# Retention and two feed-forward blocks on one core: tables formed by products, small tiles of 64 bytes, another order of products and sums

## The chip, the cores and the metric

One core of a Trainium2 chip runs the whole program. The metric is the device time of a run in microseconds, the median over several runs. The engines are TensorE (PE, the matrix products; its weight loads are PEld), VectorE (DVE), ScalarE (ACT), GpSimd (POOL) and SyncE (SP, which here only issues DMAs). Data lie in SBUF (128 partitions); products are summed in PSUM, in eight banks of 128 x 512 fp32.

## The reference

Three stages, all in fp32: retention over blocks, a feed-forward block with a squared gate, and one whose two branches are multiplied. `w_in` is 512 x 2048, `w_a` and `w_b` are 512 x 1536.

```python
Dmask = np.where(rel >= 0, lam[:, None, None] ** rel[None, :, :], 0.0)
lam_pow = lam[:, None, None] ** (pos[None, :, None] + 1)
for b in range(nb):
    intra = np.einsum('bhic,bhjc->bhij', qb, kb) * Dmask[None]
    intra = np.einsum('bhij,bhjd->bhid', intra, vb)
    inter = np.einsum('bhid,bhde->bhie', qb * lam_pow[None], kv_state)
    out[:, :, sl] = intra + inter
    kv_state = lam_block * kv_state + np.einsum('bhsd,bhse->bhde', kb_dec, vb)
...
h = x @ w_in
g = np.where(h >= 1, h, np.where(h <= -1, 0.0, (h + 1) ** 2 / 4))
x = g @ w_out
...
return (x @ w_a) * (x @ w_b) @ w_out
```

There are 2 x 768 tokens, 8 heads of 64 features and `lam` of 8 numbers, one for each head.

## The kernel before

**Tiling.** The retention runs in 12 chunks of 128 tokens (6 for each batch; a chunk here spans two blocks of the reference). The feed-forward parts run in blocks of 512 tokens, three of them (`nb`), and in tiles of 128 x 512. Each operand of a wide product is held as two fp32r tiles, a higher part `hi` and a rest `lo` (`split`, L306); one product of such pairs is three matmuls, higher by higher, higher by lower, lower by higher (`mm3`, L324). A group of two or four pairs sums into one bank by 6 or 12 matmuls. Weights come as 8-byte words and are turned into a pair by `weight` (L515): two steps on ACT, three on DVE, an add, then `split`.

**Stages.** `ready_for(c)` forms the scores of a chunk, scales its keys and values and multiplies the scores by the masks; `attention(c)` updates the state and forms the output, which is split into the block tiles. The masks `dmask` (two, of even and odd heads) and the powers for the queries `tabq` are tables of powers of lam. To make them, `lam` comes by two DMAs (`lamp` on SP, `lamb` on the ACT queue), POOL raises it to powers (`base`, L378; `kdf`, L382, the powers for the keys), `base` goes to a small DRAM tensor `rows` behind a stretch of zeros, and four DMAs on the ACT queue (L390, L394) read it back with overlapping strides, which shifts it by one in each partition. `warm` (L397) issues bf16 matmuls on zeros, 8 ahead of the first scores and 8 behind.

Then come the first feed-forward block in four groups of 512 features (`h_bank` and `gate`, L560; from the second group on `h_banks`, which forms two blocks of tokens by seven products of sums, `seven`, in place of eight), the sums over the groups (`y_bank`, `gather`), the differences of tokens that the second block needs for its seven products (`tokens_y`, `strassen_tokens`), and the second block in six groups (`ab_banks`, then `o_bank` for each block of tokens). In group g the order is ab(2g), the o products of block 2 of the group before, ab(2g+1), the o products of blocks 0 and 1 of this group.

**The order.** No order is written out for the engines. Every operation is a step of `Plan` with its ways (an engine and a cost in us), its outputs and inputs. `deadlines` gives each step a due time from the order of PE's steps; `place` walks through time, and at each point takes of the steps that can begin first the one that is due first, PE out of its next 5 steps only. It gives each step a slot of its kind of tile: `t` (24 fp32 tiles, and 14 `early` ones until the retention ends), `r` (36 fp32r, and from then on 14 `late` ones in place of the early), `raw`, and 7 banks `ps`. A step may name the lock: two SBUF operands on DVE wait in the plan until POOL's instruction ends, and the other way round. `copy` (L300) has no lock. A PE step is placed whole, behind all its inputs. The queues are then filled in this order, and each engine runs its own in order.

**Places.** Tiles lie in SBUF one behind another, each at the next multiple of 32 bytes. In the program as built the t tiles begin at byte 1152 of a partition and the r tiles at 50304, both multiples of 64 like all that follow them up to the blocks. Behind these come nine small fixed tiles (`lamp` to `half`, of 4 or 32 bytes a partition), 32 bytes apart, 288 together; then the early, later the late tiles, from byte 189856 on, which is 32 more than a multiple of 64.

The lines that the change and the steps below touch: L34 (POOLS, SHARED), L83 (`step`), L109 (`deadlines`), L130 (`place`), L300 (`copy`), L316 (`mm`), L324 (`mm3`), L338 to L399 (the tables and `warm`), L560 (`gate`), L575 (`strassen_tokens`), L675 (`y_bank`), L682 (`o_bank`), L740 and L782 (the order of the stages).

## Time and profile before

| | |
|---|---|
| median of 3 runs | 628.84 us (628.33 to 629.57) |
| the profiled execution | 631.43 us |
| its span, first to last instruction | 629.6 us |
| PE busy | 597.4 us (95%), 3060 matmuls |
| DVE, ACT, POOL busy | 418.2, 273.3, 449.8 us |
| mean granted clock of PE | 0.988 |
| chain that ended last | PE 86%, DVE 9%, DMA 3% |

The span is cut into stretches by what limits each: a start in which PE has little to do, long stretches in which PE has no idle time, and some holes between stages. PE's busy time counts overlapping records and so is no measure of how fast it works; in a stretch without holes, length over count of matmuls is. A clock of 1.00 is 2.4 GHz, 0.50 is 1.2 GHz.

### The profile page before, as it was taken

To read this page: it belongs to the slowest core of one execution; us is meant where nothing else is said; L and a number is where in the kernel's file an instruction comes from. 1 tells how busy PE (TensorE), PEld (TensorE's weight loads), DVE (VectorE), ACT (ScalarE), POOL (GpSimd) and SP (SyncE) were. 2 spreads that over 40 slices of the span, in tenths; PEclk is the share of its full clock that TensorE was granted. 3 is DMA by queue.
4 is the path that set the end of the run, shared out by engine and by line. 5 is a ranking of instruction groups with operands and counts; after the bars stand their busy time and mean duration, and the time that the engine had idled before them with its cause. 6 is when DMAs were issued, how large, how long until landed. Compare 5 with 4: busy or idle time off the path is not lost.

```text
span 629.6 us, 8361 instructions
## 1 busy us (share of the span) xinstructions
PE 597.4 (95%) x3060; PEld 477.6 (76%) x3060; DVE 418.2 (66%) x618; ACT 273.3 (43%) x480; POOL 449.8 (71%) x385
## 2 busy tenths in 40 slices
PE   5599999999899999999997989999999999999997
PEld 3478788888688878888885868878878878878875
DVE  0588635337985798569889966295774884775544
ACT  0366545446643654355744555332432523523310
POOL 3488997489776667657989979474876867758640
PEclk9699999999999999999999989999999999999999
DMA  7977401023122211221201222102111222220005
GB/s 237 304 272 244 166 2 67 1 67 101 34 68 67 87 48 68 67 82 53 68 0 68 101 81 86 35 33 68 67 68 67 68 67 68 68 68 1 0 34 200
DMA packets 21081, 52.72 MB, mean 84 GB/s; under 512 B 2600, under 2 KB 5168, under 8 KB 21040
## 3 DMA queue, kind: packets, MB, share of 16 engines
q1 hardware_dynamic: 18568, 50.86, 23.7%
q10 hardware_dynamic: 2472, 1.32, 0.8%
q8 instruction: 24, 0.39, 0.2%
q14 instruction: 17, 0.14, 0.1%
HBM read 49.03 MB, written 3.15 MB: 83 GB/s over the span
## 4 chain that ended last, share of the span: by engine, by line
PE 86%; DVE 9%; DMA 3%; issue 1%; POOL 0%; ACT 0%; SPq 0%; ACTq 0%; DVEq 0%
PE ps L319 86%; DVE t L299 3%; DVE r L299 2%; DMA t<-rows 1%; DVE block L299 1%; DMA lamp<-in_lam 1%; DMA rows<-base 1%; DVE late L299 1%; DVE r L303 1%; DVE t L563 0%; DVE t L532 0%; DVE late L303 0%; POOL base L378 0%; DVE early L299 0%; DVE block L303 0%
## 5 line engine op out<-in xcount | busy, mean ns | idle before, releaser
L299 DVE TENSOR_TENSOR t<-t,ps 128x512 f32<-128x512 f32 (+1 forms) x246 | 160.3, 666 | 124.7 <-PE ps L319 104.1
L319 PE MATMUL ps<-r,r 128*128 128x512 f32 x740 | 210.2, 394 | 7.5 <-DVE t L299 3.4
L319 PE MATMUL ps<-block,r 128*128 128x512 f32 x718 | 188.9, 393 | 2.8 <-DVE t L299 1.4
L299 POOL TENSOR_TENSOR r<-t,r 128x512 fp32r<-128x512 f32 x99 | 131.2, 1339 | 69.1 <-ACT r L303 67.5
L299 POOL TENSOR_TENSOR t<-t,t 128x512 int32<-128x512 int32 (+2 forms) x136 | 150.3, 1121 | 40.7 <-ACT r L303 18.5
L319 PEld LDWEIGHTS ps<-r,r 128*128 128x128 f32 x740 | 138.8, 188 | 41.9 <-issue 3.9
L319 PEld LDWEIGHTS ps<-block,r 128*128 128x128 f32 x718 | 134.0, 188 | 34.2 <-DVE block L299 2.2
L303 ACT CAST r<-t 128x512 fp32r<-128x512 f32 x128 | 78.2, 619 | 124.7 <-DVE t L299 71.1
L319 PE MATMUL ps<-late,r 128*128 128x512 f32 x276 | 92.4, 396 | 0.4 <-DVE r L299 0.3
L319 PE MATMUL ps<-block,late 128*128 128x512 f32 x290 | 85.0, 394 | 0.0
L319 PEld LDWEIGHTS ps<-block,late 128*128 128x128 f32 x290 | 54.4, 188 | 13.3 <-DVE t L299 0.5
L319 PE MATMUL ps<-r,late 128*128 128x512 f32 x196 | 62.1, 396 | 1.1 <-DVE late L299 0.9
L527 DVE TENSOR_SCALAR words<-words 128x512 f32<-128x512 f32 x68 | 47.3, 696 | 23.4 <-ACT words L522 22.1
L319 PEld LDWEIGHTS ps<-late,r 128*128 128x128 f32 x276 | 51.7, 188 | 13.5 <-DVE r L299 1.1
L522 ACT ACTIVATE words<-raw 128x512 f32<-128x512 f32 x68 | 43.3, 637 | 35.9 <-DVE t L532 33.3
L303 ACT CAST late<-t 128x512 fp32r<-128x512 f32 x52 | 31.7, 618 | 54.9 <-POOL t L299 31.4
L303 ACT COPY t<-ps 128x512 f32<-128x512 f32 x49 | 28.6, 586 | 47.1 <-PE ps L319 46.6
L529 DVE TENSOR_SCALAR words<-words 128x512 int32<-128x512 int32 x68 | 47.4, 697 | 1.6
L532 DVE SCALAR_TENSOR_TENSOR t<-raw,words 128x512 int32<-128x512 int32 x64 | 43.8, 684 | 2.0
L319 PEld LDWEIGHTS ps<-r,late 128*128 128x128 f32 x196 | 37.1, 189 | 10.4 <-DVE late L299 1.3
L319 PE MATMUL ps<-late,late 128*128 128x512 f32 x120 | 40.6, 402 | 1.6 <-DVE late L303 1.0
L565 ACT ACTIVATE t<-t,half 128x512 f32<-128x512 f32 x43 | 30.5, 722 | 25.8 <-DVE t L563 25.8
(78 smaller groups left out, 520.0 us busy)
## 6 DMA issues: line engine op xcount, KB each, us to landing
raw<-in_w2ab SPq DMA_DIRECT2D x24, 512.0 KB, 3.3
t<-in_att SPq DMA_DIRECT2D x37, 256.0 KB, 5.4
raw<-in_w1i SPq DMA_DIRECT2D x16, 512.0 KB, 3.4
raw<-in_w1o SPq DMA_DIRECT2D x16, 512.0 KB, 4.7
raw<-in_w2o SPq DMA_DIRECT2D x12, 512.0 KB, 3.2
early<-in_att SPq DMA_DIRECT2D x11, 256.0 KB, 5.4
out<-t SPq DMA_DIRECT2D x8, 256.0 KB, 2.3
t<-rows ACTq DMA_DIRECT2D x2, 256.0 KB, 6.4
```

Of the source, the lines that this page charges most:

```text
L299: plan.step(ways, [o], [x, y], lambda e: engine[e].tensor_tensor(out=o(), in0=x(), in1=y(), op=op))
L303: (nc.scalar.copy if e == "ACT" else nc.vector.tensor_copy)(o(), x())
L319: nc.tensor.matmul(**{k: v() if isinstance(v, View) else v for k, v in kw.items()})
L522: lambda e: nc.scalar.activation(out=words(), in_=f_(high)(), func=ACTF.Abs), horizon)
L527: lambda e: ts_(out=words(), in0=words(), scalar1=HIGH_MIN, scalar2=HIGH_MAX, op0=ALU.max, op1=ALU.min))
L529: lambda e: ts_(out=wi(), in0=wi(), scalar1=3, scalar2=0x3FFFFFFF, op0=ALU.logical_shift_left, op1=ALU.bitwise_and))
L532: lambda e: nc.vector.scalar_tensor_tensor(out=vi(), in0=high(), scalar=-0x40000000, in1=wi(), op0=ALU.bitwise_and, op1=ALU.bitwise_or))
L565: lambda e: nc.scalar.activation(out=r(), in_=r(), func=ACTF.Square, scale=0.5, bias=half()))
```

## The change

1. **Small tiles.** Each small fixed tile is 16 columns of 4 bytes (`column`), 18 of them.
2. **Tables.** `lamp`, `rows` and the DMAs around it go. POOL makes a few powers of lam (`powers8`, three strips of 32 partitions: the powers 0 to 31, 16 times as much, and differences of 16), DVE makes tables of zeros and ones by comparing running numbers (`near`, `far`), 40 small fp32 products and one more spread the powers over the partitions (banks `f1`, `f2`, `f3`, `bt`), and DVE multiplies and adds these into `dmask` (`masks`); `tabq` is a product on POOL or DVE (`query_powers`).
3. **Fillers.** `warm(40)` makes 40 steps of two bf16 matmuls that the plan may place where PE has nothing else, until the first h product is placed; those left over are dropped. They hold one bank.
4. **Order in a group.** `mm3` takes all products of higher parts first and the right-hand lower parts last; for o products the left-hand lower parts last. Each input's due time is that of its own matmul, a group may begin ahead of inputs that only later matmuls read, and the matmuls of a group are put into the order one by one.
5. **The plan.** PE is taken from its next 12 steps; `copy` on DVE names the lock; 26 t, 40 r, 8 early and late tiles; other windows for choosing among steps; a way out where the reserve of tiles lets nothing be placed.
6. **Sums in PSUM.** The last y sums of block 2 and of half of block 1 are added into the bank and split from there; the gates of the first eight h products too; one difference of tokens is formed in the bank.
7. **o products.** Two of the four o products of block 2 move behind ab(2g+1).

```diff
-POOLS = {"t": 24, "r": 36, "raw": 4, "ps": 7}
-SHARED = 14
+POOLS = {"t": 26, "r": 40, "raw": 4, "ps": 7}
+SHARED = 8
+LOOK = 12
+SPARE, SLOPE = 2, 3.0
+AHEAD = 30
+NEAR, NEAR_PE = 0.25, 0.2
...
-                    s.before.add(self.writer[k])
+                    w = self.writer[k]
+                    s.before.add(w)
+                    s.lead[w] = min(s.lead.get(w, 1e9), leads[i] if leads else 0.0)
...
+                clock += 0.0 if s.filler else s.ways[0][1]
...
-                t = min([a.late for a in s.after] + [clock + 5, bound.get(s, 1e9)])
+                t = min([a.late + a.lead[s] for a in s.after] + [clock + 5, bound.get(s, 1e9)])
...
-        pe = deque(s for s in self.steps if s.ways[0][0] == "PE")
+        pe = deque(s for s in self.steps if s.ways[0][0] == "PE" and not s.filler)
...
-                begin = max([at[e], given] + [x.done if x.engine == e else x.end + HOP for x in s.before])
+                begin = max([at[e], given] + [x.done if x.engine == e else x.end + HOP - s.lead[x] for x in s.before])
...
+                if s.filler:
+                    yield e, begin, 99, cost, s
+                    continue
...
+                choices = [x for s in ready for x in options(s, window, False)]
+                choices = [min(choices, key=lambda x: x[2])] if choices else []
...
-            near = 0.5 if e == "PE" else 0.12
+            near = NEAR_PE if e == "PE" else NEAR
...
+            if s is ends:
+                for x in [x for x in waiting if x.filler]:
+                    drop(x)
...
-        plan.step(ways or [("ACT", act(n)), ("DVE", dve(n))], [o], [x], emit)
+        plan.step(ways or [("ACT", act(n)), ("DVE", dve(n), x.buf.kind != "ps" and o.buf.kind != "ps")], [o], [x], emit)
...
+    def mm(groups, cost, outs, ins, leads=None):
+        def product(kw):
+            return lambda e: nc.tensor.matmul(**{k: v() if isinstance(v, View) else v for k, v in kw.items()})
+        s = plan.step([("PE", cost)], outs, ins, None, leads=leads)
+        s.parts = [(cost * i / len(groups), product(kw)) for i, kw in enumerate(groups)]
+        return s
...
+    def mm3(ps, pairs, start=True, late=1):
+        kws, ins, leads = [], [], []
+        for a, b in ((0, 0), (1, 0), (0, 1)) if late else ((0, 0), (0, 1), (1, 0)):
+            for l, r in pairs:
+                ins += [l[a], r[b]]
+                leads += [WIDE * len(kws)] * 2
+                kws.append(dict(out=ps, lhsT=l[a], rhs=r[b], start=(start and not kws), stop=False, skip_group_check=not start))
+        kws[-1]["stop"] = True
...
+    def column(name, dtype=F32):
+        return View(fixed([128, 16], dtype, name))
...
+    load(lamb, bass.AP(tensor=lam.tensor, offset=lam.offset, ap=[[0, 128], [1, H]]), 4096, [("ACT", 2.2, False, 4096)])
+    small("POOL", one(qi), [], lambda: nc.gpsimd.iota(one(qi)(), pattern=[[0, 1]], base=0, channel_multiplier=1), 0.14)
...
+    def power(o, e):
+        small("POOL", o, [lamb, one(e)],
+              lambda: nc.gpsimd.tensor_tensor(out=o(), in0=lamb(), in1=one(e)().to_broadcast([128, H]), op=ALU.pow), 1.64)
...
+          lambda: ts_(out=one(keep)(), in0=one(cf)(), scalar1=16.0, scalar2=None, op0=ALU.is_ge))
+    small("DVE", powers8, [powers8, one(keep)],
+          lambda: ts_(out=powers8()[64:96], in0=powers8()[64:96], scalar1=one(keep)()[64:96], scalar2=None, op0=ALU.mult))
...
+        def equal(shift):
+            o, c = new(), column(f"c{base}_{shift}")
+            small("DVE", one(c), [one(cf)],
+                  lambda: ts_(out=one(c)(), in0=one(cf)(), scalar1=float(-shift), scalar2=None, op0=ALU.add))
+            plan.step([("DVE", dve())], [o], [whole, one(c)],
+                      lambda e: ts_(out=o(), in0=whole(), scalar1=one(c)(), scalar2=None, op0=ALU.is_equal))
...
+    equal = ones_where([[1, 4], [0, 8], [1, 16]], 1)
+    near = [equal(4 * g) for g in range(4)]
+    equal = ones_where([[1, 4], [1, 8], [0, 16]], -8)
+    far = [equal(4 * g) for g in range(2)]
...
+    f1, f2, f3, bt = (bank() for _ in range(4))
+    for o, q, sel in ((f1, 1, far), (f2, 0, near), (f3, 2, near)):
+        kws = []
+        for i in range(4 * len(sel)):
+            kws.append(dict(out=o.of(lambda t, i=i: t[:, i * H:(i + 1) * H]),
+                            lhsT=sel[i // 4].of(lambda t, i=i, q=q: t[32 * q:32 * q + 32, (i % 4) * 128:(i % 4 + 1) * 128]),
+                            rhs=rows32(powers8, q), start=True, stop=True))
+        mm(kws, 0.07 * len(kws), [o], [powers8, *sel])
+    mm([dict(out=cols(bt, 0, 192), lhsT=full.of(lambda t: t[0:64, 0:128]), rhs=spread.of(lambda t: t[0:64, 0:192]),
+             start=True, stop=True)], 0.35, [bt], [full, spread])
...
-    rows = View(Buf("fixed", Slot(dram.tile([H, PITCH], F32, name="rows"))), keys=("z", "p"))
-    rbase = rows()[0:1, 0:1]
...
+    def masks(e):
+        d = dmask[e]
+        by_r = lambda v: v()[:, 0:128].rearrange("p (r a e o) -> p e a o r", a=4, e=2, o=1)[:, e].to_broadcast(shape)
+        plan.step([("DVE", dve())], [d], [far_f, f2], lambda _: nc.vector.tensor_tensor(
+            out=quad(d()), in0=far_f()[:, 0:64].rearrange("p (i a e o) -> p e a i o", a=4, e=2, o=1)[:, e].to_broadcast(shape),
+            in1=by_r(f2), op=ALU.mult))
+        near_d = new()
+        plan.step([("DVE", dve())], [near_d], [f3, dg], lambda _: nc.vector.tensor_tensor(
+            out=quad(near_d()), in0=dg()[:, 0:8].rearrange("p (b i o) -> p b i o", b=1, o=1).to_broadcast(shape),
+            in1=by_r(f3), op=ALU.mult))
+        tt(d, d, near_d, ALU.add)
...
+        sh = [64, 4, 8, 16]
+        src = lambda: broad()[r, 0:192].rearrange("p (a e n) -> p e a n", a=4, e=2)[:, e]
+        part = View(tabq.buf, lambda t: quad(t[r]), (e,))
+        plan.step([("POOL", pool(), True), ("DVE", dve(), True)], [part], [broad], lambda q: engine[q].tensor_tensor(
+            out=part(), in0=src()[:, :, 0:8].rearrange("p a (i o) -> p a i o", o=1).to_broadcast(sh),
+            in1=src()[:, :, 8:24].rearrange("p a (o r) -> p a o r", o=1).to_broadcast(sh), op=ALU.mult))
...
     def warm(n):
-        ps = bank()
-        mm([dict(out=ps, lhsT=idle.of(lambda t: t[:, 0:128]), rhs=idle, start=True, stop=True)] * n, 0.43 * n, [ps], [idle])
+        for _ in range(n):
+            s = mm([dict(out=warm_bank, lhsT=idle.of(lambda t: t[:, 0:128]), rhs=idle, start=True, stop=True)] * 2, 0.5,
+                   [warm_bank], [idle])
+            s.filler = True
...
-    def gate(ps, ft, nb):
...
+        v = ps if in_bank else r
+        tt(v, r, ps, ALU.max, ways=[("DVE", dve(), ps.buf.kind != "ps")])
+        gt[1, ft, nb] = split(v)
...
-        gate(product_in("1i", ft, nb), ft, nb)
+        gate(product_in("1i", ft, nb), ft, nb, nb < 2)
...
-        t1, t2, t3, t4 = (new() for _ in range(4))
-        for i, o, x, y in ((1, t1, y1[0], y0[0]), (2, t2, y1[1], t1), (3, t3, y1[1], y1[0]), (4, t4, y0[1], t2)):
+        t1, t3, t4 = (new() for _ in range(3))
+        t2 = y1[1] if y1[1].buf.kind == "ps" else new()
+        for i, o, x, y in ((1, t1, y1[0], y0[0]), (3, t3, y1[1], y1[0]), (2, t2, y1[1], t1), (4, t4, y0[1], t2)):
             tt(o, x, y, ALU.subtract)
         for i, o in ((2, t2), (3, t3), (1, t1), (4, t4)):
             ts[i, j] = split(o, *(x_view(1, j) if i == 1 else ()))
...
+        if g == FF1 // 512 - 1 and (nb == 2 or nb == 1 and m >= 2):
+            tt(ps, acc[("y", nb, m)], ps, ALU.add)
+            acc["y", nb, m] = ps
+            split(ps, *x_view(nb, m))
+            return
         y = gather(("y", nb, m), ps)
-        if g == FF1 // 512 - 1 and (nb != 1 or m >= 2):
+        if g == FF1 // 512 - 1 and nb == 0:
             split(y, *x_view(nb, m))
...
         r0 = nb * TB + m * 128
-        ps = mm3(bank(), [(lhs(gt[2, f, nb], m), wt["2o", f]) for f in range(2 * g, 2 * g + 2)])
...
-    warm(8)
+    warm(40)
     ready_for(0)
-    warm(8)
...
             h_bank(j, nb)
+            if c == 4:
+                ends = next(s for s in reversed(plan.steps) if s.ways[0][0] == "PE")
...
         if g:
-            for m in range(KT):
+            for m in range(2):
                 o_bank(g - 1, 2, m)
         ab_banks(2 * g + 1)
+        if g:
+            for m in range(2, KT):
+                o_bank(g - 1, 2, m)
```

## Rows read from the trace of the kernel before

**Rows 1.** Chain of waits, 0 to 60 us: start, length, what (times in us)
```profile
1.65 6.17 DMA lamp<-in_lam
...
9.55 5.14 DMA rows<-base
...
15.24 7.77 DMA t<-rows
```

**Rows 2.** Timeline of the start: start, length, engine, line, [idle before]
```profile
4.49 1.65 POOL L382 TENSOR_TENSOR kdf<-lamb,exk 128x8 f32<-128x8 f32 x1 [3.44 <-DMA lamb<-in_lam]
...
5.33 1.16 PE L319 MATMUL ps<-t,t 64*128 64x128 f32 x16 [0.88 <-DMA t<-in_att]
...
11.89 1.78 PE L319 MATMUL ps<-t,t 128*64 128x64 f32 x32 [1.28 <-POOL t L429]
...
17.10 1.04 POOL L429 TENSOR_TENSOR early<-t,kdf 128x512 f32<-128x512 f32 x1 [1.89 <-DMA t<-in_att]
...
20.64 0.69 PE L319 MATMUL ps<-early,t 128*64 128x128 f32 x2 [6.97 <-DVE early L299]
...
23.77 1.97 PE L319 MATMUL ps<-early,t 128*64 128x128 f32 x14 [2.44 <-DVE early L299]
...
25.67 2.08 PE L319 MATMUL ps<-t,t 64*128 64x128 f32 x16
```

**Rows 3.** Windows of the start: stretch, length, busy of five engines (count), clock, DMA
```profile
20.00:25.00 5.00, 1.92 (x14) 1.52 (x15) 3.07 (x5) 1.02 (x5) 1.00 (x1) 0.50 0.87 211
...
60.00:70.00 10.00, 9.53 (x110) 7.57 (x108) 8.90 (x16) 5.85 (x15) 10.00 (x9) 1.00 0.74 262
```

**Rows 4.** Windows of six stretches that PE fills, and of 166 to 630, columns as before
```profile
95.00:157.00 62.00, 62.00 (x275) 51.32 (x275) 31.48 (x48) 32.40 (x57) 46.55 (x41) 1.00 0.17 58
168.00:224.00 56.00, 56.00 (x244) 45.52 (x243) 42.15 (x65) 28.93 (x49) 40.97 (x36) 1.00 0.21 71
228.00:316.00 88.00, 88.00 (x381) 71.20 (x380) 69.07 (x104) 47.23 (x79) 64.12 (x55) 1.00 0.18 60
370.00:410.00 40.00, 40.00 (x176) 32.68 (x175) 17.09 (x26) 20.13 (x36) 29.12 (x27) 1.00 0.20 67
...
465.00:508.00 43.00, 43.00 (x187) 34.85 (x186) 26.59 (x42) 14.48 (x26) 29.69 (x27) 1.00 0.15 49
...
563.00:607.00 44.00, 44.00 (x192) 35.68 (x192) 24.60 (x38) 12.83 (x22) 28.86 (x27) 1.00 0.00 0
...
166.00:630.00 464.00, 448.02 (x1913) 358.54 (x1912) 325.15 (x467) 192.44 (x325) 323.35 (x274) 0.99 0.19 63
```

**Rows 5.** Timeline of PE alone, about 355 us, one merged run
```profile
355.65 3.11 PE L319 MATMUL ps<-block,r 128*128 128x512 f32 x13
```

**Rows 6.** Windows around holes of PE, and 346 to 361 between them
```profile
158.00:166.00 8.00, 6.03 (x25) 4.33 (x25) 7.73 (x9) 5.21 (x9) 7.14 (x6) 1.00 0.20 67
...
330.00:346.00 16.00, 11.69 (x48) 8.39 (x47) 15.76 (x18) 7.01 (x12) 14.77 (x10) 1.00 0.19 67
346.00:361.00 15.00, 15.00 (x67) 12.27 (x66) 13.84 (x22) 8.61 (x15) 14.74 (x13) 1.00 0.29 106
361.00:365.00 4.00, 2.14 (x9) 1.16 (x8) 3.93 (x4) 0.23 (x1) 3.22 (x3) 1.00 0.00 0
365.00:370.00 5.00, 5.00 (x16) 3.91 (x17) 3.75 (x6) 2.57 (x5) 3.10 (x3) 0.66 0.31 102
...
412.00:416.00 4.00, 3.13 (x13) 1.94 (x12) 3.90 (x5) 1.24 (x2) 3.84 (x5) 1.00 0.39 131
...
559.00:562.00 3.00, 1.63 (x7) 0.75 (x6) 2.97 (x3) 1.10 (x2) 2.92 (x3) 1.00 0.86 280
```

**Rows 7.** Groups of DVE, 318 to 324 us: count, busy, mean ns
```profile
L299 DVE TENSOR_TENSOR r<-t,r 128x512 fp32r<-128x512 f32 x1 | 5.7, 5743 | 0.0
L299 DVE TENSOR_TENSOR t<-t,ps 128x512 f32<-128x512 f32 x2 | 1.4, 682 | 2.1 <-PE ps L319 2.1
```

**Rows 8.** Timeline of DVE, 505 to 513 us, one cast
```profile
509.89 1.48 DVE L303 CAST r<-t 128x512 fp32r<-128x512 f32 x1
```

198 lines of the change are left out of this document (108 added, 90 removed).

## The prediction

> **What bounds the kernel now.** I read the chain of waits first, to see which engine the end hangs on. It is TensorE (PE) nearly everywhere after 23.8 us; before that it is a chain of small transfers [rows 1]. So the time is three sums: what PE idles at the start, how long one product takes in the dense stretches, and what PE idles in holes later. I read each in its own view.
>
> The start. lamp lands at 7.8 us, a power of it on POOL takes 1.65 (as the one of lamb [rows 2]), the powers go out to DRAM (5.14) and come back as tables (7.77): the last is there at 23.0 [rows 1]. The q, k and v of the first chunk are long there: PE forms its first scores at 5.33, its first state at 11.89, and then idles until 23.77, but for two matmuls [rows 2]. lamb, which comes by one transfer, is at POOL by 4.49 [rows 2]. From 20 to 25 us the granted clock is 0.50, the lower level of 1.2 GHz, because PE did nothing from 13.7 to 20.6; the 16 score matmuls that took 1.16 us at 5.33 take 2.08 at 25.67 [rows 2, 3].
>
> The dense stretches. In a window that PE fills, length over count is the interval between products. Records overlap (0.39 us each, 0.23 apart), so a window counts some 1.7 too many. 95 to 157 us: 62.00/273.3 = 226.9 ns. Later: 56/242.3 = 231.1, 88/379.3 = 232.0, 40/174.3 = 229.5, 43/185.3 = 232.1, 44/190.3 = 231.2 [rows 4]; together 271/1171.5 = 231.3. In the fast window no product reads a `late` tile. Those lie 32 bytes off a multiple of 64; r and block tiles lie on one. A busy VectorE (DVE) is no good reason: at 355.65 thirteen products without `late` take 3.11 us, (3.11 - 0.39)/12 = 227 ns, in a stretch where DVE is busy 13.84 of 15 us [rows 5, 6].
>
> The holes. PE lacks 1.97 us in 158 to 166, 4.31 in 330 to 346, 1.86 in 361 to 365, and at the ends of four later groups 0.87 in the first, 1.37 in the last, 4.7 in the four: 12.9 us in all. Behind the third of the seven the clock falls to 0.66 for 5 us, 1.7 us more [rows 6]. Why they arise is in single instructions: a DVE subtract of two SBUF tiles took 5.74 us, while those that read a bank of PSUM took 0.68 in the same stretch, and a DVE cast that the planner took for 0.69 took 1.48 [rows 7, 8]. Both stood between two SBUF tiles while POOL worked on SBUF tiles; a bank in PSUM as source spares DVE that wait.
>
> **The start after the change.** Seven transfers go: six of the ACT queue's seven, whose lamb stays, and lamp from SP's. ACT then has only computation behind its one DMA; nothing is moved past another on SP's queue. The powers are ready at 4.49 + 1.65 [rows 2], and 0.17 for the multiply by `keep`: 6.3 us. DVE makes six is_equal tiles at some 0.68 [rows 7] with small instructions, some 5 us from 1.5 on. This multiply waits for POOL, and up to three of the is_equal tiles stand behind it in DVE's order, so they may end near 9; PE's table products wait for them, with fillers and the next scores behind. The 40 table products are 80 matmuls. No row has 8 columns of output; the nearest are 32 matmuls of 64 weight columns in 1.78 us, 56 ns each [rows 2]. I take that, 4.5 us. Below lies the planner's cost, 2.8 us (its costs for other products agree with the trace); above, twice the row for twice the columns, 8.9. The Trainium skill (TensorE: Matmul & The Clock Gate, "LDWEIGHTS") has a load cost its columns over 1.2, however few rows: 107 ns here, as an estimate 8.5 us, by which the sum below would come to 608.5, on the way to rival (b).
>
> So the products end near 11.3; then on DVE near_d, the sum and the first mask at 0.68 each, 13.4; the other half 2.0 later, 15.4; and 1 us for fillers and queues, 16.4. That is 7.4 us before 23.77. But four banks hold tables and one the fillers, so the second chunk's scores (1.16) come later than now: 5.9. Fillers hold the clock: 23.77 to 27.75 at the lower level cost 2.0; I take 1.6. **Start: -7.5**, between -3 (products 8.9, clock lost) and -11. The loads are no new limit: the third chunk's keys are at POOL by 17.10 [rows 2], before PE could use them. Fewer early tiles (8 for 14, two more t) leave 34 for 38, some 15 of them tables for a while; I cost that at nothing, as the loads run ahead, and at up to 2 us in the range.
>
> **Alignment.** Every small tile is now 64 bytes, so `late` tiles come to multiples of 64. If all products take 226.9, 4.4 ns go for each of the 1913 matmuls of 166 to 630 us [rows 4]: **-8.4**. Bounds: 0, and -9.7 at the 5.1 ns of the slowest windows.
>
> **The holes.** Moving two o banks (12 products, 12 x 0.227 = 2.7 us) behind the second ab group covers four waits that are all under 2: -4.7. If the cover were gone, they come back whole. The hole at 361 has no earlier group to draw on; a view of 12 PE steps for 5, and the lock now charged to casts, should save half of 1.86 and of the clock's 1.7: -1.8. At 330 the sums stay in PSUM: their subtract on DVE takes 0.68 for sure where one took 5.74; but subtracts that POOL did go to DVE, busy 15.76 of 16 us there [rows 6]. -2.5 of 4.31; ends 0 and -4.3. At 158: -0.7, ends +1 and -2. "Higher parts first" cuts both ways: in a group of four pairs the last pair's higher part is needed at the 4th product instead of the 10th, 6 x 0.227 = 1.4 us earlier, its lower part one product later. One y stage may wait for it: +1.3 (0 to +4). **Holes: -8.4**, between -3 and -14. Gates in PSUM put eight subtracts (5.4 us) on DVE in 60 us of attention where it is busy 0.89 [rows 3]; POOL's release frees as much, so 0.
>
> **The sum.** -7.5 - 8.4 - 8.4 = -24.3. The profiled execution ran 631.43 us, span 629.6 and 1.8 around it: 607.1 for it. The median of the runs, 628.84, is 2.6 lower: **604.5 us**, of itself 599 to 610.
>
> **Rivals.** (a) The products stay slow: the offset is not the cause but the place at the top of the partition, or something else that came with these tiles. For it: no tile elsewhere has the offset, so the two can't be told apart here. Against: block tiles right below are fast. Then +8.4: 612.9; 0.11. The Trainium skill (SBUF — State Buffer, "Specifications") gives lines of 16 bytes, of which 32 is a whole number; by that the offset costs nothing and this rival holds, but no row speaks for lines of 16. (b) The tables are as late as now, by DVE's order and slow products: only 1.5 of 7.5 gained, 610.5; 0.10. (c) New holes for old: DVE has more to do around y, and the reordered groups wait for higher parts: nothing of 8.4, 612.9; 0.08. (d) All goes to its far end, -11 - 8.4 - 14.5: 595; 0.04. (e) Slower: a group may now be started ahead of its inputs, each counted on just for its own product, and lateness on the chip then stops PE inside groups. The products form 294 groups (by the code, of 6 and 12). From (24.3 + 1.3)/294 = 87 ns a group this eats everything; at 0.1 us, with all gains kept, it gives 634; 0.04. Against it: PE waits for nothing in the six windows [rows 4], so inputs are mostly long ready. (f) Nothing of it works or it cancels: 629; 0.01.
>
> **How the numbers follow.** Forecast 0.62, rivals as above. From 597 to 615 lie the forecast, (a), (b) and (c), 0.91 before what their own spreads leave out, nearer 0.8 with it. Faster by over 0.2% (1.3 us, about what a measurement here can tell): 0.62 + 0.11 + 0.10 + 0.08 + 0.04 = 0.95; within it 0.01; slower 0.04.
>
> **What would show it.** Start: the chain has no transfer but lamb, the first dense output products of chunk 0 stand near 16 us, and the clock is 1.00 from 15 to 30. Alignment: a full window late in the run gives 227 ns a product, with `late` tiles in it; 231 means rival (a). Holes: no idle of PE over 0.3 us at the ends of the ab groups but the first; the y sums' subtracts on DVE all near 0.68. I am wrong if PE shows many idles of a tenth of a us inside groups (e), if DVE is full through 20 to 80 us with PE waiting for it, or if the first mask comes after 20 us.

## The result, and the profile after

The changed kernel takes **615.14 us**, median of 4 runs (614.73 to 615.42), beside 628.94 (628.33 to 629.57) in 4 runs of the kernel before on the same chip: a ratio of 0.978 (0.9763 to 0.9797). It is faster, as forecast, but by 13.8 us where 24.3 were forecast, and the time lies just past the far end of the range. The profiled execution took 615.42 us, its span is 613.6 (before 629.6).

The three terms of the forecast come out in one account. There are 2340 wide products (128x512 outputs). From their starts in the trace I read when the 301st begins (the start with the retention behind it), and sum for the next 2000, to 599.7 us, what each interval takes over 226.7 ns: in "products" where it follows without a gap in under 300 ns, in "holes" else (gaps, and the stretches at the lower clock behind them). The part behind the 2301st is 9.5 us in one and 9.3 in the other.

| | 301st begins | products | holes | PE ends | span |
|---|---|---|---|---|---|
| before | 134.5 | +8.2 | +19.4 | 625.0 | 629.6 |
| after | 142.1 | +4.2 | 0.0 | 609.0 | 613.6 |
| difference | **+7.6** | **-4.0** | **-19.4** | -16.0 | -16.0 |
| forecast | -7.5 | -8.4 | -8.4 | | -24.3 |

So every term was missed: the start has become worse by as much as it was to become better, products gained half, and holes gave more than twice what I counted. The profiled execution of the kernel before took 631.43 us, 2.5 more than the median; in two later forms of it that keep its order (64-byte tiles, 1248 bytes of padding) the holes come to 17.1, so some 2 of the 19.4 us seem to belong to this one execution. The chain of waits of the changed kernel (start, length, what) shows the last: behind PE's first instruction at 6.01 there is one break of over 0.1 us, before 93.70, inside the retention.

```profile
5.88 0.14 issue
6.01 62.05 PE ps L347 x592
68.06 0.01 issue
68.06 25.07 PE ps L347 x272
...
93.22 0.43 DVE t L328
93.66 0.04 issue
93.70 515.35 PE ps L347 x2276
```

The start, as the timeline of PE shows it (start, length, engine, line, operation, count, [idle before]):

```profile
6.01 2.08 PE L347 MATMUL ps<-t,t 64*128 64x128 f32 x16 [6.01 <-DMA t<-in_att]
8.02 3.58 PE L347 MATMUL ps<-powers,t 32*128 32x8 f32 x16
11.53 2.08 PE L347 MATMUL ps<-t,t 64*128 64x128 f32 x16
13.53 12.99 PE L347 MATMUL ps<-powers,t 32*128 32x8 f32 x64
26.45 1.00 PE L347 MATMUL ps<-early,t 64*128 64x192 f32 x2
27.39 5.21 PE L347 MATMUL ps<-early 128*128 128x512 bf16 x14
32.52 0.69 PE L347 MATMUL ps<-t,early 128*64 128x64 f32 x16
```

From 6.01 on PE is never idle, and yet it is late. The 80 table products take 3.58 + 12.99 = 16.6 us, 12.99/64 = 203 ns each on the mean; by their starts in the trace they follow each other in 213 ns, but for the few where one strip ends and the next begins. The 16 scores take 2.08 as in the stretch before that had the lower clock, for 1.16 at the upper [rows 2, 3]: PE works here at 1.2 GHz. The fillers, which were to hold the clock, come only at 27.39. The reason stands in DVE's timeline: the zeros that they multiply are written by its last small instruction, and DVE then waits 10.7 us for the tables:

```profile
9.65 0.27 DVE L391 MEMSET early<- 128x256 uint32 x1
20.63 1.28 DVE L486 TENSOR_TENSOR early<-t,ps 128x512 f32<-128x512 f32 x2 [10.71 <-PE ps L347]
```

Windows of PE's stretches (stretch, length, busy of PE, PEld, DVE, ACT, POOL with counts, clock, DMA) answer [rows 4]:

```profile
100.00:150.00 50.00, 50.00 (x222) 41.42 (x221) 20.64 (x31) 27.07 (x46) 43.77 (x39) 1.00 0.12 43
170.00:225.00 55.00, 55.00 (x243) 45.23 (x242) 42.27 (x63) 28.71 (x49) 42.48 (x37) 1.00 0.23 77
230.00:315.00 85.00, 85.00 (x373) 69.73 (x372) 63.34 (x99) 45.61 (x76) 62.73 (x54) 1.00 0.19 62
166.00:606.00 440.00, 440.00 (x1925) 361.37 (x1924) 287.07 (x438) 201.34 (x339) 332.72 (x288) 1.00 0.19 64
```

Counted as in the prediction, 50.00/220.3 = 227.0 ns, then 227.9 and 85/371.3 = 228.9; before it was 226.9, 231.1 and 232.0. From 166 us to the end of the wide products PE is busy all the time, at the full clock: nothing is left of [rows 6].

### The profile page after: what moved, and what is told of

It is laid out like the page before. It is cut to its first block, busy times and chain, and to the rows that moved or that the text cites. A ratio compares the mean times of both kernels' runs of the same rounds, so it can differ in the third digit from the quotient of the medians.

```text
span 613.6 us, 8555 instructions
## 1 busy us (share of the span) xinstructions
PE 602.4 (98%) x3140; PEld 494.8 (81%) x3140; DVE 389.4 (63%) x621; ACT 283.7 (46%) x498; POOL 453.2 (74%) x397
## 4 chain that ended last, share of the span: by engine, by line
PE 98%; DMA 1%; DVE 0%; issue 0%; SPq 0%; DVEq 0%
PE ps L347 98%; DMA t<-in_att 1%; DVE t L328 0%; SPq L343 0%; DVEq L971 0%; DVEq L328 0%
## 5 line engine op out<-in xcount | busy, mean ns | idle before, releaser
L347 PE MATMUL ps<-r,r 128*128 128x512 f32 x984 | 270.1, 390 | 0.0
L328 POOL TENSOR_TENSOR r<-t,r 128x512 fp32r<-128x512 f32 x152 | 195.7, 1304 | 79.6 <-ACT r L332 74.6
L347 PEld LDWEIGHTS ps<-r,r 128*128 128x128 f32 x984 | 184.8, 188 | 40.1 <-issue 0.2
L347 PE MATMUL ps<-block,r 128*128 128x512 f32 x892 | 216.3, 391 | 0.0
L347 PEld LDWEIGHTS ps<-block,r 128*128 128x128 f32 x892 | 166.8, 188 | 36.1 <-issue 0.5
L332 ACT COPY t<-ps 128x512 f32<-128x512 f32 (+3 forms) x58 | 33.0, 569 | 82.2 <-PE ps L347 81.7
L640 ACT ACTIVATE t<-raw 128x512 int32<-128x512 uint32 x66 | 41.8, 665 | 0.0
L347 PE MATMUL ps<-t,t 64*128 64x128 f32 (+3 forms) x504 | 33.3, 279 | 6.6 <-DMA t<-in_att 6.0
L347 PEld LDWEIGHTS ps<-t,t 128*64 128x64 f32 (+2 forms) x504 | 28.1, 159 | 11.8 <-issue 9.3
L347 PE MATMUL ps<-block,late 128*128 128x512 f32 x116 | 30.9, 395 | 0.0
```

Source lines behind the costliest of these rows:

```text
L328: plan.step(ways, [o], [x, y], lambda e: engine[e].tensor_tensor(out=o(), in0=x(), in1=y(), op=op))
L332: (nc.scalar.copy if e == "ACT" else nc.vector.tensor_copy)(o(), x())
L347: return lambda e: nc.tensor.matmul(**{k: v() if isinstance(v, View) else v for k, v in kw.items()})
L640: lambda e: nc.scalar.activation(out=c(), in_=low.of(lambda t: t.bitcast(U32))(), func=ACTF.Copy, scale=2.0**-29), horizon)
```

## The experiments

Times are of the same sort as above; "before" beside them was 629.39 to 630.18 throughout.

### The start

**Tables made as before.** The changed kernel with the old way through DRAM, in small tiles of 64 bytes.

```diff
-    power(powers8, ef)
...
-    f1, f2, f3, bt = (bank() for _ in range(4))
...
+    load(lamp, bass.AP(tensor=lam.tensor, offset=lam.offset, ap=[[1, H], [0, 16], [1, 1]]), 512)
...
+    rz, rp = View(rows.buf, keys=("z",)), View(rows.buf, keys=("p",))
...
+    warm_bank = bank()
```

> The changed kernel with the tables made as before: powers to DRAM and read back (small tiles stay 64 bytes, fillers stay). If the 80 table matmuls of 128 weight columns hold up the start (17 us of PE in the changed kernel), the first output products come near 24 us again instead of 32.5 and the time falls by 7 to 9 us, to 606 to 608. If the start doesn't set the end, because DVE is busy 0.88 between 40 and 92 us, it stays within 2 us of 615.

Measured: 604.73 us (604.12 to 607.84), ratio 0.9616 (0.959 to 0.9643), 10.4 us less than the changed kernel. The 301st product begins at 132.1 for 142.1, which is nearly all of it. The table part of the change, with the late fillers that it brings, is a loss of 10 us: here the zeros stand early in DVE's order again, and the first fillers run at 1.19. Its chain of waits shows that the old way is also faster here than it was before [rows 1]: 4.28 and 4.79 us for the two transfers that took 5.14 and 7.77, and PE runs from 18.64.

```profile
0.74 4.96 DMA lamp<-in_lam
...
8.64 4.28 DMA rows<-base
...
13.01 4.79 DMA t<-rows
...
18.64 203.44 PE ps L347 x1360
```

**Zeros first.** DVE writes the zeros ahead of everything else, so that fillers can run early.

```diff
-    small("DVE", idle, [], lambda: nc.vector.memset(idle(), 0.0), 0.3)
-    small("DVE", one(ci), [one(qi)],
...
+    def first():
+        nc.vector.memset(idle(), 0.0)
+        ts_(out=one(ci)(), in0=one(qi)(), scalar1=31, scalar2=None, op0=ALU.bitwise_and)
+
+    small("DVE", [idle, one(ci)], [one(qi)], first, 0.47)
```

> The changed kernel with one step moved: the zeros that the fillers read are written first on DVE (at about 1 us instead of 9.65), so that ten fillers run ahead of the first table products. If the table products took 213 ns each because PE stood at the lower of its two clocks, they take 107 and the time falls by 80 x 0.107 = 8.5 us, to 606.6. If 213 ns is what 128 fp32 weight columns cost at either clock, or if the clock falls again in the table products, it stays at 615.

Measured: 610.7 us (608.23 to 616.26), ratio 0.9713 (0.9662 to 0.9765); span 608.1. PE's timeline and the windows of the same kernel:

```profile
6.02 1.16 PE L347 MATMUL ps<-t,t 64*128 64x128 f32 x16 [0.77 <-DMA t<-in_att]
7.11 1.95 PE L347 MATMUL ps<-powers,t 32*128 32x8 f32 x16
...
11.16 9.70 PE L347 MATMUL ps<-powers,t 32*128 32x8 f32 x64
```

```profile
10.00:15.00 5.00, 5.00 (x54) 4.45 (x50) 0.00 (x1) 0.00 (x0) 2.59 (x3) 0.98 1.06 399
15.00:20.00 5.00, 5.00 (x25) 5.00 (x25) 1.28 (x2) 0.00 (x0) 0.00 (x0) 0.50 1.02 402
```

and windows of the table products alone (stretch, length, busy of PE with count, clock, DMA):

```profile
11.20:14.50 3.30, 3.30 (x32) 1.00 1.05 397
16.00:20.00 4.00, 4.00 (x20) 0.50 1.02 401
```

Scores now take 1.16. A table product's record is 0.25 us long at the upper level and 0.36 at the lower, and a window counts each that it touches: (3.30 + 0.25)/32 = 111 ns and (4.00 + 0.36)/20 = 218, to one product more or less; from start to start the trace has 112 and 213 ns. But PE does nothing but such products from 11.16 on, and from 15 to 20 us the granted clock is 0.50. So the price at the upper level would be 80 x 0.112 = 9.0 us, at the far end that I gave (8.9), and the lower clock nearly doubles it.

**Strips interleaved.** The products of the three strips of 32 partitions take turns in one step.

```diff
-    for o, q, sel in ((f1, 1, far), (f2, 0, near), (f3, 2, near)):
-        kws = []
-        for i in range(4 * len(sel)):
...
+    kws = []
+    for i in range(16):
+        for o, q, sel in ((f2, 0, near), (f3, 2, near), (f1, 1, far)):
```

> The changed kernel with the 40 table products as one step, those of the three 32-partition strips in turn instead of one strip behind the other. If products of different strips run beside each other, 80 matmuls take 32 turns at 213 ns, some 7 us instead of 17, and the time falls by 8 to 10 us to 605 to 607. If weight loads of strips stand in one line, 17 us and 615 stay.

Measured: 605.87 us (604.1 to 606.18), ratio 0.9618 (0.9591 to 0.9645). The 80 products take 7.00 us for 16.6, though still without early fillers:

```profile
9.70 7.00 PE L347 MATMUL ps<-powers,t 32*128 32x8 f32 x80
16.62 1.00 PE L347 MATMUL ps<-t,t 64*128 64x192 f32 x2
18.04 4.54 PE L347 MATMUL ps<-early 128*128 128x512 bf16 x14 [0.41 <-DVE t L491]
22.51 1.15 PE L347 MATMUL ps<-t,early 128*64 128x64 f32 x32
```

88 ns each in place of 207. By the starts in the trace a turn of three products, or of two when the third strip has run out, takes the 213 ns that one product took before, at the same lower level: products of different strips overlap, and products of one strip do so less, if at all. The Trainium skill (TensorEngine Tiling (Array Packing), "Key Properties") says that tiles of the array load weights and multiply in parallel; the 213 ns for a whole turn agree.

### The time of a product

**The kernel before with small tiles of 64 bytes.** Nothing else of the change; `late` tiles come to multiples of 64.

```diff
-    lamp = View(fixed([128, 1], F32, "lamp"))
+    lamp = View(fixed([128, 16], F32, "lamp"), lambda t: t[:, 0:1])
...
-    half = View(fixed([128, 1], F32, "half"))
+    half = View(fixed([128, 16], F32, "half"), lambda t: t[:, 0:1])
```

> The kernel before, with its nine small tiles made 64 bytes each and nothing else: late tiles then begin at multiples of 64. If the offset of 32 bytes makes the products slow, all wide products take 227 ns and the time falls by 8.4 us to 620.5. If it is the place at the top of the partition (rival a of the prediction), the late stretches keep 231 ns and the time stays at 629.

**The changed kernel with all tiles moved by 32 bytes.**

```diff
+    pad = const.tile([128, 8], F32, name="pad")
     free = {
```

> The changed kernel with one unused tile of 32 bytes ahead of all others, so that every t, r, block and late tile lies 32 bytes off a multiple of 64. If the offset is the cause, all 2340 wide products take 231 to 232 ns, 4.6 to 5.2 more: 615.1 + 10.8 to 12.2, 626 to 627. If the place is, 615.

Measured: 630.09 us (628.03 to 632.1, 10 runs), ratio 1.0008 (0.9993 to 1.0024), and 615.18 us (614.79 to 616.23), the changed kernel's own time. Neither does anything; products cost +8.1 us over the least in the first (before: +8.2) and +4.2 in the second. Multiples of 64 are not the cause, and my alignment step is wrong.

**128 and 384 bytes of padding behind the blocks.** The changed kernel's late tiles stand 1152 bytes of small tiles behind the blocks, 4.5 times 256. With 384 more it is 1536 = 3 x 512, with 128 more 1280 = 5 x 256.

```diff
+    pad = const.tile([128, 96], F32, name="pad")
```

> The changed kernel with an unused tile of 384 bytes behind the blocks, so that the small tiles take 1536 bytes, a multiple of 512, and late tiles stand to the 512-byte pieces of r and block tiles as these stand to each other. If products are slow where their two streams of reads, or those of the next load, stand at different offsets within 512 bytes, all take 226.7 ns and the time falls by 2340 x 2.0 ns = 4.7 us to 610.4. If late tiles are slow for another reason (that they come from a pool opened in the midst of the program), 228.7 stays, and 615.

```diff
+    pad = const.tile([128, 32], F32, name="pad")
```

> The same with 128 bytes, 1280 in all: a multiple of 256 and not of 512. Products with late tiles at 226.7 would say that 256 bytes is the step that matters, at 231 to 234 that it is 512. By the theory of a reopened pool they stay slow in both.

Measured: 611.64 us (610.91 to 611.85), ratio 0.9714 (0.9695 to 0.9733), and 610.49 in one run. In both every wide product from 120 us on takes 226.7 ns, and the products' excess is 0.0. The windows from 230 to 315 us, of the kernel before with 64-byte tiles:

```profile
230.00:315.00 85.00, 85.00 (x370) 68.99 (x369) 65.87 (x99) 46.84 (x78) 64.35 (x55) 1.00 0.19 62
```

and of the changed kernel with 384 bytes:

```profile
230.00:315.00 85.00, 85.00 (x377) 70.38 (x376) 64.38 (x100) 46.52 (x77) 63.57 (x55) 1.00 0.18 62
```

85/368.3 = 230.8 ns against 85/375.3 = 226.5; the changed kernel itself had 373 (the windows shown above). As 1280 is no multiple of 512, the step is 256 bytes or a divisor of 256 above 128: 256. An offset of all tiles together does nothing, so it is the place of the late tiles to the others that counts. In the changed kernel (first) and with 384 bytes (second) the same products run in the same order; where late and r tiles alternate as moving operand, 36 products, the rows begin and end so:

```profile
191.68 0.40 PE L347 MATMUL ps<-late,r 128*128 128x512 f32 x1
191.92 0.39 PE L347 MATMUL ps<-r,r 128*128 128x512 f32 x1
...
199.94 0.40 PE L347 MATMUL ps<-late,r 128*128 128x512 f32 x1
```

```profile
191.83 0.39 PE L348 MATMUL ps<-late,r 128*128 128x512 f32 x1
192.06 0.39 PE L348 MATMUL ps<-r,r 128*128 128x512 f32 x1
...
199.99 0.39 PE L348 MATMUL ps<-late,r 128*128 128x512 f32 x1
```

8.26/36 = 229.4 against 8.16/36 = 226.7 ns. By their starts, each of the 15 products with a late operand in the first stretch takes 234 ns and each of the others 226 or 227.

**The kernel before with 1248 bytes of padding**, so that its small tiles with it are 1536 bytes.

```diff
+    pad = const.tile([128, 312], F32, name="pad")
```

> The kernel before with 1248 bytes of padding behind the blocks, so that its late tiles too stand at a whole multiple of 256 bytes from the r and block tiles, and nothing else. If the offset of the two operands of a product to one another modulo 256 bytes is what costs (as the padded forms of the changed kernel say): every wide product from 120 us on at 226.7 ns, 8.2 us less for the 2000 products behind the first 300, 620.5 to 622.5 us. If it is not (something else in the changed kernel made its padded forms fast): 629 to 631 us.

Measured: 620.29 us in one run, 9.9 less than one run of before beside it. Its window answers the 232.0 ns of [rows 4]:

```profile
228.00:316.00 88.00, 88.00 (x390) 72.88 (x389) 69.40 (x104) 49.48 (x82) 67.19 (x57) 1.00 0.18 60
```

88/388.3 = 226.6 ns. Products cost +0.4 us for +8.2, which is 7.8 of the 9.9. The holes came to 17.1, as in the run with 64-byte tiles, which gained nothing, so the other 2 us are a matter of single executions and not shown to come from the padding. One line of padding has nearly the alignment term that I forecast, in a kernel with none of the change.

Why then did the change gain 4.0 us on products? By fewer mixed ones, with one late operand and one other. Of the 2000 products the trace names 738 of them before and 429 after. 8.2/738 and 4.2/429 us are 11.1 and 9.8 ns for each: about the same, though the offset went from 32 bytes off a multiple of 256 to 128 off. This is a mean and no price of one product. In the kernel before, products of two late tiles, which lie whole multiples of 2048 bytes apart, took 231.8 ns (100 of them, at most six in a row), and those of two r tiles 230.6; in the changed kernel a product without a late operand took 232 where the next one's weights came from a late tile (80 of them). So the lost time also falls on the neighbours of a mixed product, and that it acts between the two operands of one product is not shown; that it goes with the offset is.

### The holes

**Four parts alone, each undone in the changed kernel.** No lock on casts:

```diff
-        plan.step(ways or [("ACT", act(n)), ("DVE", dve(n), x.buf.kind != "ps" and o.buf.kind != "ps")], [o], [x], emit)
+        plan.step(ways or [("ACT", act(n)), ("DVE", dve(n))], [o], [x], emit)
```

> The changed kernel with the lock taken off copies in the plan, as before. If the lock in the plan is what closed the holes at the ends of the ab groups (a cast on DVE took 1.48 us in place of 0.69 while POOL worked), idles of PE of 0.3 to 1 us come back there, 3 us or more in all; if other parts closed them, PE's idle stays under 1 us behind the start.

The o products unmoved and the last y sums from SBUF:

```diff
-        if g == FF1 // 512 - 1 and (nb == 2 or nb == 1 and m >= 2):
-            tt(ps, acc[("y", nb, m)], ps, ALU.add)
...
-            for m in range(2):
+            for m in range(KT):
                 o_bank(g - 1, 2, m)
...
-        if g:
-            for m in range(2, KT):
-                o_bank(g - 1, 2, m)
```

> The changed kernel with two parts taken back: the o products are not moved (all four behind the first half of a group), and the last y sums are taken and split from SBUF as before. The two parts act at different places: the ends of the ab groups (after 350 us) for the o move, and the y sums near 320 to 335 us. Theory (the two parts closed the holes, as the prediction has it): TensorE idles again about 4.7 us at the ends of the later groups and 2 to 4 us near 330, and the run takes 619 to 624 us. Rival (the order of the higher parts and the wider view of the planner closed them, and the two parts were not needed): no idle over 0.5 us at either place, 615 us. If one place has its holes and the other not, that one part alone did its work.

The order of products in a group:

```diff
-        for a, b in ((0, 0), (1, 0), (0, 1)) if late else ((0, 0), (0, 1), (1, 0)):
-            for l, r in pairs:
+        for l, r in pairs:
+            for a, b in ((0, 0), (0, 1), (1, 0)):
```

> The changed kernel with the order of products inside a group as before (all three products of one pair, then the next pair), each input still counted on for its own product. Theory (higher parts first is a small loss of at most 1.3 us, or nothing, as the prediction costs it): 614 to 615 us, no idle of TensorE over 0.5 us behind the start. Rival (higher parts first gives lower parts time and is what closed the holes): idle of 2 us or more in all near 160, 330 and 361 us, 617 to 621 us.

The view of PE's next steps:

```diff
-LOOK = 12
+LOOK = 5
```

> The changed kernel with the planner's view of TensorE steps at 5 as before, for 12. Theory of the prediction (the wider view gives TensorE other work at the holes of 158 and 361 us, some 2 to 3 us with the clock): idle there again, 616 to 619 us. Rival (the other parts close them by themselves): no idle over 0.7 us, 615 us.

Measured, one run each, with the account of above:

| undone | us | 301st | products | holes |
|---|---|---|---|---|
| nothing (after) | 615.14 | 142.1 | +4.2 | 0.0 |
| lock on casts | 615.51 | 142.2 | +4.2 | 0.0 |
| o move and y sums | 618.96 | 142.0 | +4.0 | +3.8 |
| order in a group | 614.56 | 141.6 | +4.0 | 0.0 |
| view of 12 | 617.69 | 142.5 | +4.7 | +1.1 |

Undone alone, the lock and the order change nothing. With o move and y sums undone, PE idles at four places, two near 337 and two near 363 us, and nowhere at the ends of the later groups. The windows:

```profile
335.00:340.00 5.00, 3.75 (x15) 2.33 (x14) 3.28 (x4) 1.74 (x3) 5.00 (x5) 1.00 0.00 0
...
361.00:366.00 5.00, 3.65 (x16) 2.48 (x15) 3.96 (x5) 3.09 (x6) 4.11 (x4) 1.00 0.03 10
```

So the y sums are worth some 3.8 us, as expected of them, and the o move, to which I gave 4.7, nothing: its holes don't come back without it, with the new numbers of buffers. The view gives 0.6 us of idle at 360 us and 1.1 in all. Some 14 of the 19.4 us were still without a cause.

**Halves.** All parts of the work undone (o move, y sums, gates in their bank, order of the token differences, order in a group), the planner as changed; and the planner undone in five places (due times by product, view, nearness, lock, numbers of buffers), the work as changed. The lines beyond those shown:

```diff
-        gate(product_in("1i", ft, nb), ft, nb, nb < 2)
+        gate(product_in("1i", ft, nb), ft, nb)
...
-        t1, t3, t4 = (new() for _ in range(3))
-        t2 = y1[1] if y1[1].buf.kind == "ps" else new()
+        t1, t2, t3, t4 = (new() for _ in range(4))
```

> The changed kernel with all parts of the work itself that bear on waits taken back together: o products unmoved, last y sums from SBUF, gate products kept in SBUF instead of their bank, the four token differences in the old order, products of a pair kept together in a group. The planner stays as changed. Holes and stretches at the lower clock behind the first 300 wide products cost 19.4 us in the kernel before and nothing in the changed one. Theory A (what the work reads and writes made the holes, as the prediction has it): 10 us or more of the 19.4 come back, 625 us or more. Theory B (the planner made them, by what it counted on): about what the two parts taken back before cost, 3 to 5 us, 618 to 621 us.

```diff
-POOLS = {"t": 26, "r": 40, "raw": 4, "ps": 7}
-SHARED = 8
+POOLS = {"t": 24, "r": 36, "raw": 4, "ps": 7}
+SHARED = 14
-LOOK = 12
+LOOK = 5
-NEAR, NEAR_PE = 0.25, 0.2
+NEAR, NEAR_PE = 0.12, 0.5
-        mm(kws, WIDE * len(kws), [ps], ins, leads)
+        mm(kws, WIDE * len(kws), [ps], ins)
```

> The counterpart: the work as changed, the planner as before in five places: each input counted on at the start of its group, a view of 5 TensorE steps, nearness 0.12 and 0.5, no lock on casts, 24 and 36 buffers with 14 that change hands. Theory A (the work itself): no holes worth more than 3 us, 615 to 618 us. Theory B (the planner): 10 us or more of holes, 625 us or more. Both below 5 us: either half suffices.

**Three parts of the planner alone:** due times by product (`leads` left out of the last line above), nearness, and the numbers of buffers (the first four lines above).

> The changed kernel with each input counted on at the start of its group instead of at its own product, nothing else. If the counting by product is the part of the planner that closes holes (theory B): 5 us or more of TensorE idle at the places of the old holes, 621 us or more. If not: 615 to 617 us. By the prediction's rival (e) it could even gain, as groups would not be started ahead of inputs: not expected, since TensorE idles only 0.6 us behind the start.

> The changed kernel with the planner's two nearness limits as before (0.12 us for the other engines, 0.5 for TensorE, against 0.25 and 0.2), nothing else: which of the steps that could start soon goes first, by due time. If this choice closed the holes: 619 us or more. If not: 614 to 616 us.

> The changed kernel with the numbers of buffers as before (24 t, 36 r, of them 14 that change hands, for 26, 40 and 8), nothing else. It is the one of the five planner parts undone together (628.1 us of span, 9.6 us of holes, 7.5 of them from 152 to 178 us) that no run has undone alone. If fewer buffers made those holes: 5 us or more of them near 152 to 178 us, and with 14 late tiles products at some 230.5 ns (8 us in all over the least, for 4.2): 623 to 628 us. If it takes two parts together: no hole over 1 us, only the products slower, 617 to 620 us.

Measured, one run each:

| undone | us | 301st | products | holes |
|---|---|---|---|---|
| the work, five parts | 619.74 | 141.0 | +5.5 | +4.2 |
| the planner, five places | 629.89 | 143.1 | +8.2 | +9.5 |
| due times by product | 617.18 | 141.4 | +6.6 | +0.1 |
| nearness | 620.66 | 144.5 | +6.4 | +0.7 |
| numbers of buffers | **629.12** | 143.2 | +8.3 | +8.5 |

The planner's half outweighs the work's, and of it nearly all is three numbers: 26 t, 40 r and 8 shared tiles for 24, 36 and 14. Undone alone they lose 14.0 us, more than expected (629.12 us for 623 to 628) and as much as the whole change gains (13.8). The two halves bring back 4.2 and 9.5 us of holes, 13.7 of the 17.1 to 19.4 before; what closed the rest no run shows. Due times and nearness cost 2 to 5 us, but not by holes (0.7 at most): the plan falls out so that more products have one late operand (531 and 551 for 429), and with the old nearness the retention ends 2.4 us later, 1.4 of it a wait for a transfer. Nearness did reach the time that I had set for "closed the holes", but without holes, so it didn't close them.

What the buffers do stands in the windows, here of the changed kernel:

```profile
120.00:130.00 10.00, 10.00 (x46) 8.28 (x45) 4.80 (x8) 6.75 (x12) 9.92 (x9) 1.00 0.31 104
130.00:140.00 10.00, 10.00 (x46) 8.29 (x45) 0.00 (x0) 3.83 (x7) 9.72 (x9) 1.00 0.01 2
...
172.00:178.00 6.00, 6.00 (x28) 4.99 (x27) 5.67 (x7) 3.37 (x6) 4.64 (x4) 1.00 0.00 0
```

and of the same with the old numbers, with PE's timeline behind:

```profile
120.00:130.00 10.00, 10.00 (x46) 8.27 (x45) 1.30 (x2) 3.93 (x7) 7.37 (x8) 1.00 0.00 0
130.00:140.00 10.00, 10.00 (x45) 8.04 (x44) 0.00 (x0) 0.00 (x0) 0.00 (x0) 1.00 0.01 2
...
172.00:178.00 6.00, 3.62 (x13) 2.61 (x12) 6.00 (x11) 5.92 (x10) 5.64 (x5) 0.86 0.29 89
```

```profile
175.09 1.94 PE L347 MATMUL ps<-block,r 128*128 128x512 f32 x6 [2.38 <-DVE t L328]
```

With the old numbers DVE, ACT and POOL all stand still for the ten us from 130 to 140, while PE has long work; 40 us later all three are full and PE waits for DVE. With the new ones POOL goes on, 9.72 of 10 us, and PE waits for nothing at 172. The kernel before has a pause of the same sort ten us earlier, and holes from 158 on:

```profile
120.00:130.00 10.00, 10.00 (x46) 8.28 (x45) 0.00 (x0) 3.30 (x6) 2.29 (x2) 1.00 0.01 2
```

So the three numbers make the holes, and I take it that the work which PE waited for could have been done in the pause ahead, had there been free tiles. This last step is argued: the two kernels differ by the numbers alone, but in the trace DVE and ACT wait there for PE's banks and POOL for DVE, and no run shows which tiles were taken, nor which of the three numbers does it.

### The causes mended together

Strips interleaved, zeros first, 128 bytes of padding, and six steps of fillers for 40:

```diff
+    pad = const.tile([128, 32], F32, name="pad")
...
+    def first():
...
+        for o, q, sel in ((f2, 0, near), (f3, 2, near), (f1, 1, far)):
...
-    warm(40)
+    warm(6)
```

> The changed kernel with the three causes found so far mended together: the table products of the three strips of 32 partitions interleaved, the zeros for the fillers written first so that fillers run ahead of the tables, and 128 bytes of padding behind the blocks so that all tiles stand at whole multiples of 256 bytes to one another. Theory (the three gains are of different places and add): from the run with interleaved strips, 605.9 us, padding takes 3.5 to 4.5 us, and table products at the upper clock with the fillers done earlier take 2 to 5 us: 597 to 600 us, dense products from 17 to 20 us, every wide product at 226.7 ns from 120 us on. Rival (what TensorE gains at the start is lost again as it waits for DVE's masks, or for loads that come no earlier): the gain of the start is 0 to 1 us, 601 to 602 us, with idle of TensorE behind the tables.

Measured: **594.97 us** (594.64 to 595.48, 4 runs), ratio 0.945 (0.9435 to 0.9466), better than expected. Products +0.0, holes 0.0, the 301st begins at 125.7, 6.6 us earlier than with the strips alone and 6.4 earlier than with the tables made as before: mended, the new tables are worth having. PE's timeline:

```profile
1.33 4.45 PE L348 MATMUL ps<-t 128*128 128x512 bf16 x10 [1.33 <-DVE ci L394]
...
9.32 3.74 PE L348 MATMUL ps<-powers,t 32*128 32x8 f32 x80
12.99 0.59 PE L348 MATMUL ps<-early,t 64*128 64x192 f32 x2
14.04 1.93 PE L348 MATMUL ps<-t,early 128*64 128x64 f32 x32 [0.45 <-issue]
```

The 80 products take 3.74 us, 47 ns each or 112 a turn, and end 3.6 us earlier than with strips alone; the 14 fillers that then ran behind the tables (4.54 us) are gone from there. The clock is not held throughout: it falls to 0.69 from 13 to 16 us, behind the table products. Against before: 125.7 - 134.5 = -8.8 at the start, -8.2 products, -19.4 holes, 36.4 of the 36.7 us between the spans (34.6 between the medians).

## Why the prediction was right or wrong

**Start: wrong by 15 us, at the price of the table products.** I took 80 x 56 ns = 4.5 us from the row of 32 matmuls with 64 weight columns; the trace has 16.6. That row was the nearest, but in three ways it was not near: half the columns, outputs of 64 columns for 8, and the full clock. At the upper level one costs 112 ns (zeros first), 9.0 us in all, already my far end; at the lower 213, and PE stood at the lower. The other failed step is in the same part: "Fillers hold the clock". I costed the fillers, but not what they wait for. Their zeros stand last among DVE's small instructions and so the fillers last in PE's order, behind the tables. Nor do early fillers hold the clock through a long run of such products: with the zeros first it was 0.50 from 15 to 20 us. The Trainium skill's rule for weight loads (TensorE: Matmul & The Clock Gate, "LDWEIGHTS"), 107 ns for 128 columns, was nearer than my row. The trace agrees with it within 5 ns at the upper level (112), and takes twice that at the lower (213). The steps around it held: the powers ready at 7.0 (6.3), and 6.0 us from the last table product to the next outputs of PE (26.5 to 32.5) for 5.1. With strips, zeros and fillers mended the term comes to -8.8, for -7.5. The first outputs, which I looked for near 16 us at a clock of 1.00, came behind 32.5. Rival (b), tables as late as now, was right in kind and too mild: they came later than now.

**Alignment: half the gain, by another cause.** "In the fast window no product reads a `late` tile" was right, and that the offset matters too. Wrong was the modulus: not 64 bytes for each tile by itself but 256 for the late tiles to the others. The change moved them to 128 off, where they cost about what they had cost, and rival (a), products stay slow, held for the mixed products (11.1 and 9.8 ns on the mean). That the sum fell by 4.0 came from fewer late tiles, an edit that I had weighed only at the start. By the Trainium skill's lines of 16 bytes (SBUF — State Buffer, "Specifications") no such offset should cost anything; 229.4 against 226.7 ns for the same 36 products decides against that as the whole of it. I had said that the two causes can't be told apart in the trace of before; one padded run of that kernel does it.

**Holes: right in sign, less than half in size.** I read 12.9 us in seven holes and 1.7 of clock; the account has 15.7 of gaps and 3.7 of slow stretches. The 12.9 was all of PE's idle time, but records of products overlap by 0.16 us, so each of the 17 gaps costs that much more from start to start, 2.8 in all: I had taken the overlap into the dense stretches and not into the holes. The other 2.0 us beyond the clock's 1.7 lie mostly in the first product behind a gap, some 0.1 us each. The larger error is in what closes them. The step that failed is the cost of the buffers: "Fewer early tiles ... I cost that at nothing". The 8.5 us of holes and 4.1 of products that come with the old numbers make it the largest of the edits that were undone alone, and I looked for its effect only at the start, in loads. I had sought the cause where PE waited, in single slow DVE instructions [rows 7, 8], and not some 30 to 40 us ahead, where DVE was idle. The y sums (about 3.8) were near their term of -2.5, the o move (-4.7) was worth nothing that a run shows, order in a group 0 for +1.3, the wider view 1.1 for 1.8; the hole at 361, which I gave to the view alone, comes back with the y sums too (1.35 us at 361 to 366). Rival (e), stalls inside groups, is refuted: PE idles 0.6 us behind the start, and due times by product cost nothing of that sort.

The time came within a tenth of a per cent of the far end because two misses of 15 and 11 us had opposite signs; the range was no judge of the steps.

## What to carry to other kernels

Price many small products by a row with the same columns, the same strip and the same clock, or by bounds that span all three, and ask of work that is to keep the clock up what it itself waits for. Where an engine waits for a full one, look back for the stretch in which that one was idle, and ask which buffers kept it so: the numbers of buffers moved this kernel more than any change to its work. When products differ by some ns with the names of their tiles, pad between the groups of tiles, by 32 to 384 bytes, and look again before telling a cause.

## What the runs showed of the hardware

- A 128x512 fp32r product took 226.7 ns where all tiles that products read lay whole multiples of 256 bytes apart in the partition. Where the late tiles were 32, 64 or 128 bytes off that, 2000 products lost 4 to 8 us in all, some 10 to 13 ns for each with one late operand, part of it on its neighbours; moving all tiles by 32 bytes changed nothing.
- Products of 32 rows, 128 weight columns and 8 output columns followed each other in one strip in 112 ns at the granted clock of 1.00 and 213 at 0.50; with strips in turn, a turn of two or three products took the same 112 (80 products in 3.74 us).
- The granted clock fell to 0.50 while PE did nothing but such products (15 to 20 us, with zeros first).
- The windows of the changed kernel give a clock of 1.00 for its first 30 us, in which scores took their length of the lower level: there the length of a known instruction tells the level, and the clock column does not.
